# Attention with routed experts: two gathers, one copy, one eviction and the lead expert's gates stand at other places

## Chip, cores and metric

One Trainium2 chip, one core. The metric is device time in microseconds (us), the median of several runs of one launch. The engines are called as in the profile: PE is TensorE's matmul, PEld its weight load, DVE is VectorE, ACT is ScalarE, POOL is GpSimd, SP is SyncE (it only issues DMAs here).

## What is computed

A sparse attention over 8 batches, 8 heads, 576 positions and head size 64, in float32, whose output rows (4608 tokens of 512 numbers) go to one of 8 experts each.

```python
x = attention(q, k, v).transpose(0, 2, 1, 3).reshape(4608, 512)   # heads 0-3 a local mask, 4-7 a strided one
logits = x @ w_gate
e_idx = argmax(logits, axis=1)
gate_w = softmax(logits)[arange(N), e_idx]
eom = sigmoid(x @ w_output_gate)
for e in range(8):
    mask = e_idx == e
    h = maximum(x[mask] @ w1[e], 0)          # 512 -> 1024
    out[mask] = gate_w[mask, None] * eom[mask, e, None] * (h @ w2[e])
```

## The kernel before

The kernel has two parts. The first is the attention, 40 steps `t` (8 batches of `NS` = 5 steps) that run as a software pipeline: in step `t` the scores of step `t` are multiplied, the probabilities of `t - 2` are transposed, the values of `t - 3` are multiplied, and the rows of `t - 4` are transposed for the routing and written to DRAM (`xd`). Within a step the code calls `pump(place)` at numbered places; there the side work (`logits`, `gating`, `pick`, `ahead`, written as generators) goes on until it yields the next place. So the order on each engine is the order in which this Python loop issues instructions, and a waiting instruction holds up all that stand behind it on its engine.

Side work of the attention that the change touches:

- `ahead` (L475): behind batch 3 an expert is picked as the lead expert; two gathers (`fetch`, an indirect DMA that POOL issues, L157) bring 256 of its rows from `xd` into `xg`; two steps before the end of the loop PE transposes them (L497) and ACT copies them to `xe` (L500).
- `lead_layer` (L505): the lead expert's first layer on these 256 rows, 32 float32 matmuls (L530; the trace counts two records for each) in four pairs of output blocks. It serves as filler: `fill(n)` issues n of the 32. The pairs use two PSUM banks in turn; a pair is emptied by ACT (relu to `hha`, L514) and DVE (the remainder to `hla`, L515), both issued by `flush`. While `hold[0]` is true a finished pair is not emptied unless its bank is needed; after the last matmul one more call of `fill` issues the emptying of the last pair.
- `even` (L228): copies the values shifted by one block to `vev`, in quarters; the strided steps of a batch multiply with it (L334).
- `gating` (L547): routing weights, slots, and the two tables `hit` (L738, L739) and `named` (L703) from which PE makes `book` (`place`, L599; `enter`, L606). For the last batch it ends the attention: `place` of the row numbers, `tokens_first` (the indices `idx0` of the first gathers of the experts), then `weights`, `parted` (the weight in three bfloat16 parts, L696 and L698), three more `named`, `place`, `enter` and `count` (L441, L442).

The second part is `experts`. It splits the lead expert's weights in a high and a low float32r part (ACT L1003, DVE L1004), runs the second layer of the lead expert's 256 rows (`by_token`, L1124, 24 matmuls for each of two blocks of 128), then eight ranks, of which each has eight groups of layer 1 (`layer1`, L1086) and a layer 2. `gates` gives the weights of all rows, `store` scales a result by its weight on ACT (L1211) and scatters it with POOL (L1212). `rank` and `by_rank` sort the experts by load and make the indices of the gathers. A group of layer 1 writes one of four PSUM tiles `hp`; the lead expert's results stand in two tiles `yp`, which are next written in rank 0's layer 2.

Of the kernel before, what the change touches and what calls it, by code (L numbers as in the profile page):

```python
# [20 lines left out]
E = 8  # L21
# [38 lines left out]
def attn_moe_kernel(  # L60
# [111 lines left out]
    def attention():  # L172
        with ExitStack() as actx:
# [304 lines left out]
            def ahead():  # L478

                def loads():  # L480
                    for c in range(4):
                        load_w(0, 1, cs=[c])
                        yield (8, 4, 3, 0)[c]

                chains.append([loads(), clock[0] + 1, None])
                for c in range(EH // 128):
                    while now[0] % NS != 1:
                        yield 0, 3
                    xgs[c] = xg_p.tile([128, DM], F32, name="xg")
                    fetch(xgs[c], xd[0:EB * S, :], tabe[:, c:c + 1], EB * S - 1)  # L490
                    yield 0, 4 if c == 0 else 3
                for c in range(EH // 128):
                    while now[0] < ns - 2 + c:
                        yield 0, 3
                    tp = ps_g.tile([128, 512], F32, name="gp")
                    for k in range(KC):
                        nc.tensor.transpose(out=tp[:, 128 * k:128 * (k + 1)], in_=xgs[c][:, 128 * k:128 * (k + 1)],  # L497
                                            identity=ident)
                    yield 0, 4
                    nc.scalar.copy(out=xe[:, :, 128 * c:128 * (c + 1)], in_=tp.rearrange("p (k t) -> p k t", k=KC))  # L500
                    if c + 1 < EH // 128:
                        yield 0, 3
                fillers.append(lead_layer())
# [40 lines left out]
            def gating(b, j0, j1, ci):  # L544
# [191 lines left out]
                else:  # L736
                    V.tensor_tensor(out=pos[:, 1, :], in0=dst, in1=lo, op=ALU.subtract)
                    V.tensor_tensor(out=low, in0=many(lows, slice(0, n)), in1=wide(lo, 128), op=ALU.is_equal)  # L738
                    V.tensor_tensor(out=high, in0=many(highs, slice(0, n)), in1=wide(pos[:, 1, :], nh), op=ALU.is_equal)  # L739
                    for v in range(2):  # L740
                        name(v)
# [91 lines left out]
            def shifted(t):  # L833
# [6 lines left out]
                last = [(c, nc.vector, 1, 1)] if c == B - 1 and k == 2 else []  # L840
                return [(c, nc.scalar, k // 2, k % 2)] + last
# [4 lines left out]
            while t < ns:  # L846
# [40 lines left out]
                at(expo, 0)  # L887
                if t in WIPES:
                    wipe(*WIPES[t])
# [91 lines left out]
    def by_rank():  # L981
        pick = sq[:, 0].unsqueeze(2).to_broadcast([128, E, HB, E])
        page = moe.tile([128, E, HB], F32, name="page")
        nc.vector.scalar_tensor_tensor(out=page, in0=book[:, 0], scalar=float(QB), in1=book[:, 1], op0=ALU.mult, op1=ALU.add)
        for v, w in enumerate((page, gate)):
            nc.vector.tensor_tensor(out=own, in0=w.rearrange("p e k -> p k e").unsqueeze(1).to_broadcast([128, E, HB, E]),
                                    in1=pick, op=ALU.mult)
            nc.vector.tensor_reduce(out=pages[:, v], in_=own, axis=AX.X, op=ALU.add)
            if v == 0:
                nc.vector.tensor_scalar(out=pages[:, 0], in0=pages[:, 0], scalar1=float(N), scalar2=None, op0=ALU.add)  # L990
                nc.vector.tensor_copy(out=idx, in_=pages[:, 0])
# [367 lines left out]
    def experts():  # L1359
# [5 lines left out]
        gates()  # L1365
# [6 lines left out]
        by_token(0, 0, 128, lead_gate[:, 0:1], tabe[:, 0:1], lag=2)()  # L1372
# [4 lines left out]
        sent = [by_token(0, 128 * c, 128, lead_gate[:, c:c + 1], tabe[:, c:c + 1], between) for c in range(1, EH // 128)]  # L1377
        hs.append(tuple(moe.tile([128, FC, WHB], F32R, name=n) for n in ("hhb", "hlb")))
        for fn in sent:
            fn()  # L1380
        for r in range(E):
            nxt = r + 1 < E
            if r == 0:
                rank()
                by_rank()
# [8 lines left out]
            for j in range(FC):  # L1394
                layer1(r, j)
                if r == 0 and j == 1:
                    count_spare()
                    send_away()
# [117 lines left out]
```

## Time and profile before

| what | us |
|---|---|
| median of 3 runs (603.65, 604.36, 608.99) | 604.36 |
| profiled execution, whole | 609.73 |
| its span, first to last instruction | 607.8 |
| PE busy in it (96%) | 583.0 |
| DVE busy (52%) | 313.8 |
| ACT busy (46%) | 281.2 |
| POOL busy (32%) | 195.4 |

The profile is of one execution, 5.4 us above the median. A row of the timeline gives the start, the duration, the engine, the line, the operation and `out<-in` with the tiles' names, then how often it is repeated and, in brackets, how long the engine stood idle before it and what ended that. The attention fills the first 178 us, the experts the rest. From 205 us on PE is busy without a gap but for small ones near 495, 535 and 564 us, so a gap of PE before that moves the end.

### The profile page before, as it was taken

Reading aid. Unit: us, or ns where it says so; the run is one execution under the profiler, and the core shown is the slowest. Engines: PE = TensorE matmul, PEld = TensorE weight load, DVE = VectorE, ACT = ScalarE, POOL = GpSimd, SP = SyncE. Lnnn points to the kernel's source line nnn. Section 1 sums busy time; section 2 is a strip of 40 time slices with the busy share of each in tenths; the row PEclk is TensorE's granted clock in tenths of the full one; section 3 lists DMA queues with packets and bytes.
Section 4 is the critical chain, followed back from the end, with each engine's and each line's share of the span. In section 5 each row is a group of like instructions: output and inputs, shape, how many; then the busy total and the mean of one; then the engine's idle time right before and its main releaser. Section 6 shows DMA issues by size and latency. Waiting matters only on the chain. (4 is left out here: it accounts for less than half of the span.)

```text
span 607.8 us, 14522 instructions
## 1 busy us (share of the span) xinstructions
PE 583.0 (96%) x5670; PEld 492.2 (81%) x5670; DVE 313.8 (52%) x706; ACT 281.2 (46%) x553; POOL 195.4 (32%) x275
## 2 busy tenths in 40 slices
PE   7898999997989999999999999999999999999996
PEld 5676777766768989988998899889978878888875
DVE  4876989899589453443243324333532452452420
ACT  3886778786335344333333334243333442452430
POOL 4325766778321325011400140125021422311011
PEclk9998999999999999999999999999999999999998
DMA  9998898888432845053314331445055355352001
GB/s 315 315 304 262 285 294 280 262 293 252 135 126 87 324 159 175 24 171 132 121 35 163 135 121 35 148 143 149 3 184 156 94 175 142 103 179 83 19 8 52
DMA packets 42488, 97.93 MB, mean 161 GB/s; under 512 B 5458, under 2 KB 16346, under 8 KB 42394
## 3 DMA queue, kind: packets, MB, share of 16 engines
q1 hardware_dynamic: 34122, 73.47, 37.3%
q0 software_dynamic: 6864, 19.74, 9.8%
q10 hardware_dynamic: 1408, 3.38, 1.5%
q8 instruction: 71, 1.16, 0.8%
q14 instruction: 23, 0.19, 0.1%
HBM read 77.74 MB, written 20.58 MB: 162 GB/s over the span
## 5 line engine op out<-in xcount | busy, mean ns | idle before, releaser
L1086 PE MATMUL hp<-xh,w1h 128*128 128x256 f32 (+8 forms) x384 | 127.0, 331 | 1.1 <-ACTq L1292 1.1
L1086 PE MATMUL hp<-xl,w1h 128*128 128x256 f32 (+8 forms) x384 | 126.9, 331 | 0.1
L1086 PE MATMUL hp<-xh,w1l 128*128 128x256 f32 (+8 forms) x384 | 126.8, 330 | 0.0
L1124 PE MATMUL yp<-w2h,hhb 128*128 128x512 f32 (+1 forms) x208 | 83.2, 400 | 0.0
L1124 PE MATMUL yp<-w2l,hhb 128*128 128x512 f32 (+1 forms) x208 | 81.2, 391 | 0.0
L1124 PE MATMUL yp<-w2h,hlb 128*128 128x512 f32 (+1 forms) x208 | 81.1, 390 | 0.0
L1086 PEld LDWEIGHTS hp<-xh,w1h 128*128 128x128 f32 x384 | 72.6, 189 | 4.8 <-ACTq L1292 1.4
L1212 POOL DMA_INDIRECT out_dram<-ys,idx x32 | 32.9, 1030 | 132.4 <-ACT ys L1211 132.4
L1086 PEld LDWEIGHTS hp<-xl,w1h 128*128 128x128 f32 x384 | 72.6, 189 | 3.3 <-DVE xl L1004 0.4
L1212 POOL DMA_INDIRECT out_dram<-ys,ri x18 | 20.5, 1139 | 170.2 <-ACT ys L1211 167.2
L1086 PEld LDWEIGHTS hp<-xh,w1l 128*128 128x128 f32 x384 | 72.6, 189 | 2.8
L1004 DVE TENSOR_TENSOR xl<-tp,xh 128x512 fp32r<-128x512 f32 (+3 forms) x40 | 25.8, 650 | 85.4 <-ACT xh L1003 85.4
L1003 ACT CAST xh<-tp 128x512 fp32r<-128x512 f32 (+3 forms) x40 | 22.0, 556 | 99.6 <-PE tp L1063 99.6
L1109 DVE SCALAR_TENSOR_TENSOR hlb<-hp,hhb 128x384 fp32r<-128x384 f32 (+3 forms) x48 | 28.3, 591 | 67.3 <-ACT hf L1108 67.3
L1106 ACT ACTIVATE hhb<-hp 128x384 fp32r<-128x384 f32 (+3 forms) x48 | 24.8, 518 | 79.4 <-PE hp L1086 75.3
L308 POOL TENSOR_TENSOR p_t<-p_t,st 128x512 f32<-128x512 f32 x40 | 42.0, 1050 | 44.7 <-DVE rs L347 18.9
L157 POOL DMA_INDIRECT xg<-xd,idx x40 | 43.6, 1090 | 23.5 <-DVE idx L455 9.4
L1124 PEld LDWEIGHTS yp<-w2l,hhb 128*128 128x128 f32 (+1 forms) x208 | 38.8, 187 | 8.6
L1211 ACT ACTIVATE ys<-yp,pages 128x512 f32<-128x512 f32 (+1 forms) x36 | 24.9, 693 | 45.0 <-issue 35.5
L1124 PEld LDWEIGHTS yp<-w2h,hhb 128*128 128x128 f32 (+1 forms) x208 | 38.9, 187 | 8.1 <-issue 0.4
L1004 DVE TENSOR_TENSOR w1l<-raw,w1h 128x1024 fp32r<-128x1024 f32 x32 | 39.1, 1225 | 11.9 <-ACT w1h L1003 11.7
L1124 PEld LDWEIGHTS yp<-w2h,hlb 128*128 128x128 f32 (+1 forms) x208 | 38.9, 187 | 7.7
(216 smaller groups left out, 1078.7 us busy)
## 6 DMA issues: line engine op xcount, KB each, us to landing
raw<-in_moe_w_dram SPq DMA_DIRECT2D x54, 512.0 KB
vst<-in_vs_dram SPq DMA_DIRECT2D x8, 780.0 KB
vlt<-in_vl_dram SPq DMA_DIRECT2D x16, 292.5 KB
q_t<-in_ql_dram SPq DMA_DIRECT2D x8, 576.0 KB
q_t<-in_qs_dram SPq DMA_DIRECT2D x7, 650.0 KB
xd<-x_t SPq DMA_DIRECT2D x80, 54.0 KB
xd<-x_t SPq DMA_DIRECT2D x16, 256.0 KB
raw<-in_moe_w_dram ACTq DMA_DIRECT2D x6, 512.0 KB
```

What stands on the lines that cost most here:

```text
L157: nc.gpsimd.indirect_dma_start(out=dst, out_offset=None, in_=src, in_offset=bass.IndirectOffsetOnAxis(ap=idx, axis=0), bounds_check=top, o ...
L308: nc.gpsimd.tensor_tensor(out=p_t, in0=p_t, in1=st, op=ALU.subtract)
L1003: nc.scalar.copy(out=hi, in_=src)
L1004: nc.vector.tensor_tensor(out=lo, in0=src, in1=f32(hi), op=ALU.subtract)
L1086: nc.tensor.matmul(out=hp[:, 0:n], lhsT=w[:, k, 128 * j:128 * (j + 1)], rhs=x[:, k, 0:n], start=first, stop=(k == KC - 1 and w is w1l))
L1106: nc.scalar.activation(out=hh[:, j, 0:s], in_=hp[:, 0:s], func=AF.Relu)
L1109: nc.vector.scalar_tensor_tensor(out=hl[:, j, 0:s], in0=hp[:, 0:s], scalar=0.0, in1=f32(hh[:, j, 0:s]), op0=ALU.max, op1=ALU.subtract)
L1124: nc.tensor.matmul(out=yp[0:m, :], lhsT=h[:, j, o:o + m], rhs=w[:, j, :], start=(n == 0), stop=(n == len(order) - 1))
L1211: nc.scalar.activation(out=ys[0:m, 0:n], in_=yp[0:m, 0:n], func=AF.Copy, scale=w[0:m, :])
L1212: i = nc.gpsimd.indirect_dma_start(out=out.rearrange("t (k d) -> (t k) d", k=k), out_offset=bass.IndirectOffsetOnAxis(ap=row, axis=0), in_ ...
```

## The change

The change has five edits. (1) The two gathers of `ahead` stand at other places of the same step, 4 and 5 for 3 and 4. (2) The last quarter of the last batch's `even`, which was an extra copy on DVE in step 39, is made by ACT, behind the exponential of that step. (3) In the last batch's `gating` a `fill(1)` with the hold lifted stands between the table `hit` and the first two `named`. (4) `gates` and the two `store` of the lead expert are issued behind rank 0's first group of layer 1. (5) `by_rank` comes in two halves: the indices ahead of rank 0's groups as before, the weights behind its second group; `count_spare` and `send_away` move from behind the second to behind the third.

```diff
@@ ahead
                     while now[0] % NS != 1:
-                        yield 0, 3
+                        yield 0, 4
                     xgs[c] = xg_p.tile([128, DM], F32, name="xg")
                     fetch(xgs[c], xd[0:EB * S, :], tabe[:, c:c + 1], EB * S - 1)
-                    yield 0, 4 if c == 0 else 3
+                    yield 0, 5 if c == 0 else 3
@@ gating
                     V.tensor_tensor(out=high, in0=many(highs, slice(0, n)), in1=wide(pos[:, 1, :], nh), op=ALU.is_equal)
+                    if last:
+                        hold[0] = False
+                        fill(1)
+                        hold[0] = True
                     for v in range(2):
                         name(v)
@@ shifted
-                last = [(c, nc.vector, 1, 1)] if c == B - 1 and k == 2 else []
-                return [(c, nc.scalar, k // 2, k % 2)] + last
+                return [(c, nc.scalar, k // 2, k % 2)]
@@ the loop over t
                 at(expo, 0)
+                if t == ns - 1:
+                    even(B - 1, nc.scalar, 1, 1)
@@ by_rank
-    def by_rank():
+    def by_rank(v):
...
-        for v, w in enumerate((page, gate)):
...
+        w = moe.tile([128, E, HB], F32, name="page") if v == 0 else gate
@@ experts
-        gates()
         first_spare()
...
-        by_token(0, 0, 128, lead_gate[:, 0:1], tabe[:, 0:1], lag=2)()
+        sent = [by_token(0, 0, 128, lead_gate[:, 0:1], tabe[:, 0:1], lag=2)]
...
-        for fn in sent:
-            fn()
...
                 rank()
-                by_rank()
+                by_rank(0)
...
                 layer1(r, j)
+                if r == 0 and j == 0:
+                    gates()
+                    for fn in sent:
+                        fn()
                 if r == 0 and j == 1:
+                    by_rank(1)
+                if r == 0 and j == 2:
                     count_spare()
                     send_away()
```

Where it moves rows, `-` is before and `+` is the changed kernel. On POOL, in step 36 of the attention (the two gathers are L157; `named` is the table of an earlier batch):

```order
 L703 TENSOR_TENSOR named<-hit,parts 96x6x48
 L308 TENSOR_TENSOR p_t<-p_t,st 128x512
-L157 DMA xg<-xd,tabe 128x512
-L703 TENSOR_TENSOR named<-hit,parts 96x6x48 x2
-L157 DMA xg<-xd,tabe 128x512
+L703 TENSOR_TENSOR named<-hit,parts 96x6x48 x2
+L157 DMA xg<-xd,tabe 128x512 x2
 L308 TENSOR_TENSOR p_t<-p_t,st 128x512
```

The two `named` stand ahead of the first gather now, not behind it.

On DVE, in the last batch's gating (the `hit` table, an emptying L515 of the lead expert's layer, `named`):

```order
 L738 TENSOR_TENSOR hit<-hcst,lo 96x6x128
 L739 TENSOR_TENSOR hit<-hcst,pos 96x6x48
+L515 SCALAR_TENSOR_TENSOR hla<-sp,hha 128x512
 L703 TENSOR_TENSOR named<-hit,hcst 96x6x48 x2
 L606 TENSOR_TENSOR book<-book,gp 128x240
```

One emptying stands ahead of the first `named`. Some 15 rows later on the same engine, between the counts (L577, L586) and `parted` (L696, L698):

```order
 L577 TENSOR_REDUCE s_3468<-oh 96x8
 L586 TENSOR_TENSOR cum<-cum,s_3468 96x8
-L515 SCALAR_TENSOR_TENSOR hla<-sp,hha 128x512
+L515 SCALAR_TENSOR_TENSOR hla<-sp,hha 128x512 x2
 L696 CAST parts<-wall 96x6
 L698 TENSOR_TENSOR rest<-wall,parts 96x6
```

Two emptyings stand ahead of `parted` where one did; the second is that of the last pair, which before was DVE's last row of the attention. The reason is the count: the loop still calls `fill(10)` there, but one matmul has been issued earlier, so nine are left and the tenth call issues the last emptying.

On ACT, in step 39, the exponential (L312), the copy of the transposed probabilities (L325) and the gating's exponential (L618):

```order
 L425 COPY lg<-gp 128x288
 L312 ACTIVATE p_t<-p_t 128x512
+L232 COPY vev<-vlt_133 64x1040
 L325 COPY pt<-tp 128x512
 L618 ACTIVATE dd<-dd 96x48
```

The last quarter of `vev` stands between two copies of ACT; on DVE the same L232 is gone.

## Rows read from the trace of the kernel before

**Rows 1.** The page, part 1: busy us, share of the span, instructions.

```profile
PE 583.0 (96%) x5670; PEld 492.2 (81%) x5670; DVE 313.8 (52%) x706; ACT 281.2 (46%) x553; POOL 195.4 (32%) x275
```

**Rows 2.** PE's waits in the whole span: us in total, times, longest us.

```profile
PE xp L334 <- issue: 2.7, 2, 2.4
PE gp L430 <- ACT p_t L312: 2.0, 1, 2.0
...
PE sp L266 <- DMA hha<-in_ks_dram: 1.5, 1, 1.5
```

**Rows 3.** Ten-us stretches: busy us of each engine, granted clock, DMA share, GB/s.

```profile
0.00:10.00 10.00, 7.28 (x60) 5.11 (x64) 3.69 (x5) 3.52 (x3) 4.29 (x10) 1.00 0.85 265
...
40.00:50.00 10.00, 7.61 (x161) 6.05 (x163) 7.53 (x25) 4.68 (x13) 2.88 (x3) 0.91 0.83 270
...
150.00:160.00 10.00, 10.00 (x142) 7.90 (x140) 7.39 (x26) 3.08 (x10) 2.58 (x6) 0.83 0.25 73
...
170.00:180.00 10.00, 7.59 (x43) 5.89 (x42) 8.68 (x30) 2.71 (x4) 4.08 (x4) 1.00 0.30 88
```

**Rows 4.** Timeline of POOL around the two gathers: start, duration, then the instruction.

```profile
135.89 1.16 POOL L157 DMA_INDIRECT xg<-xd,tabe  x1 [0.17 <-DMA xd<-x_t]
137.09 1.29 POOL L703 TENSOR_TENSOR named<-hit,parts 96x288 bf16<-96x288 bf16 x2
138.55 1.04 POOL L157 DMA_INDIRECT xg<-xd,tabe  x1 [0.17 <-DVE rs L347]
```

**Rows 5.** Timeline of PE, 138 to 150 us.

```profile
138.43 0.78 PE L599 MATMUL gp<-named,hit 96*128 96x240 bf16 x6 [1.08 <-POOL named L703]
...
142.13 0.60 PE L497 MATMUL gp<-ident,xg 128*128 128x128 f32 x4
...
149.72 0.51 PE L430 MATMUL gp<-ident,lg 128*96 128x128 f32 x3 [2.04 <-ACT p_t L312]
```

**Rows 6.** Line L157 from 130 to 150 us: issue to landing.

```profile
DMA to landing us min/median/max: 5.7/5.8/5.9
```

**Rows 7.** DMA issues: times, then median us to landing.

```profile
xg<-xd,idx POOLq DMA_INDIRECT x40, 3.7
```

**Rows 8.** Timeline of DVE, 145 to 150 us.

```profile
145.75 2.06 DVE L232 COPY vev<-vlt 64x1040 f32<-64x1040 f32 x1
```

**Rows 9.** Timeline of ACT, 142 to 149 us.

```profile
142.77 0.58 ACT L500 COPY xe<-gp 128x512 f32<-128x512 f32 x1 [0.62 <-PE gp L497]
...
146.99 1.06 ACT L232 COPY vev<-vlt 64x1040 f32<-64x1040 f32 x1
...
148.62 0.44 ACT L425 COPY lg<-gp 128x288 f32<-128x288 f32 x1
```

**Rows 10.** Timeline of PE, 171 to 180 us.

```profile
171.79 0.43 PE L599 MATMUL gp<-named,hit 96*128 96x96 bf16 x6 [0.66 <-DVE named L703]
...
174.13 3.72 PE L530 MATMUL sp<-xe,raw 128*128 128x256 f32 x16 [0.55 <-DVE hla L515]
...
179.47 0.50 PE L1124 MATMUL yp<-w2h,hha 128*128 128x512 f32 x1 [1.21 <-ACT w2h L1003]
```

**Rows 11.** Timeline of ACT, 177 to 186 us.

```profile
177.89 0.60 ACT L514 ACTIVATE hha<-sp 128x512 fp32r<-128x512 f32 x1 [3.12 <-PE sp L530]
...
185.65 0.69 ACT L1211 ACTIVATE ys<-yp,lead_gate 128x512 f32<-128x512 f32 x1 [0.77 <-DVE spare L1262]
```

**Rows 12.** Timeline of DVE, 173 to 193 us.

```profile
173.39 0.69 DVE L515 SCALAR_TENSOR_TENSOR hla<-sp,hha 128x512 fp32r<-128x512 f32 x1
...
175.41 0.16 DVE L696 CAST parts<-wall 96x6 bf16<-96x6 f32 x1
...
176.42 1.25 DVE L703 TENSOR_TENSOR named<-hit,parts 96x288 bf16<-96x288 bf16 x3
...
179.45 2.36 DVE L1004 TENSOR_TENSOR w2l<-hhb,w2h 128x1024 fp32r<-128x1024 f32 x2 [0.18 <-ACT w2h L1003]
...
191.94 1.21 DVE L1004 TENSOR_TENSOR xl<-tp,xh 128x512 fp32r<-128x512 f32 x2
```

More of the change, by code (lines that the diff above doesn't have):

```diff
@@ L979, in gates @@
         nc.vector.tensor_reduce(out=lead_gate, in_=own[:, 0, 0:n], axis=AX.X, op=ALU.add)
-    def by_rank():
+    def by_rank(v):
         pick = sq[:, 0].unsqueeze(2).to_broadcast([128, E, HB, E])
-        page = moe.tile([128, E, HB], F32, name="page")
-        nc.vector.scalar_tensor_tensor(out=page, in0=book[:, 0], scalar=float(QB), in1=book[:, 1], op0=ALU.mult, op1=ALU.add)
-        for v, w in enumerate((page, gate)):
[L986 to L991, printed above, removed]
+        w = moe.tile([128, E, HB], F32, name="page") if v == 0 else gate
+        if v == 0:
+            nc.vector.scalar_tensor_tensor(out=w, in0=book[:, 0], scalar=float(QB), in1=book[:, 1], op0=ALU.mult, op1=ALU.add)
+        nc.vector.tensor_tensor(out=own, in0=w.rearrange("p e k -> p k e").unsqueeze(1).to_broadcast([128, E, HB, E]),
+                                in1=pick, op=ALU.mult)
+        nc.vector.tensor_reduce(out=pages[:, v], in_=own, axis=AX.X, op=ALU.add)
+        if v == 0:
+            nc.vector.tensor_scalar(out=pages[:, 0], in0=pages[:, 0], scalar1=float(N), scalar2=None, op0=ALU.add)
+            nc.vector.tensor_copy(out=idx, in_=pages[:, 0])
     def copied():
@@ L1376, in experts @@
             between[TURN_AT[c - 2]].append((split_w, 0, 1, c))
-        sent = [by_token(0, 128 * c, 128, lead_gate[:, c:c + 1], tabe[:, c:c + 1], between) for c in range(1, EH // 128)]
+        sent += [by_token(0, 128 * c, 128, lead_gate[:, c:c + 1], tabe[:, c:c + 1], between) for c in range(1, EH // 128)]
         hs.append(tuple(moe.tile([128, FC, WHB], F32R, name=n) for n in ("hhb", "hlb")))
-        for fn in sent:
-            fn()
         for r in range(E):
```

## The prediction

> **What bounds the kernel.** I read the page first: PE is busy 583.0 of 607.8 us [rows 1], and the experts' part keeps it busy nearly without a gap, so only what opens or closes a gap of PE in the attention and at its end can move the time. PE's waits come next: its longest three are 2.4, 2.0 and 1.5 us [rows 2]. Last the stretches of 10 us, for the clock: after the idle 2.4 us (at 45 us) and 2.0 us (at 148 us) the mean granted clock fell to 0.91 and 0.83, while it stayed at 1.00 in the stretch with the idle 1.5 us (at 5 us) and in that from 170 us, with three shorter ones [rows 3]. A fall is to the lower of the two levels (1.2 of 2.4 GHz); 0.83 over 10 us is 1.7 us of full clock lost. So a gap of 2 us costs its length and up to 1.7 us more.
>
> The profiled execution took 609.73 us, 5.4 above the median of 604.36. The idle 2.4 us "issue" in L334 and the lower clock behind it (together about 4 us) are what I suspect of this difference, since no tile is waited for there, but the other runs have no trace. The sum below is of differences, made on the profiled execution and then put on the median.
>
> **Edit 1, the gathers.** Before, the first gather stands at 135.89 us, the two `named` behind it end at 137.09 + 1.29 = 138.38, and PE, idle for 1.08 us, starts L599 at 138.43 [rows 4, 5]. With the `named` first (from 135.72, the gather's start less its 0.17 of idle) they end at 137.0; PE was free at 138.43 - 1.08 = 137.35, so this gap is gone. The first gather starts 1.3 us later, at 137.2; the second stays at about 138.55, and POOL is free as before. But PE needs the first gather at L497, 142.13 us. Issue to landing took 5.7 to 5.9 us here [rows 6]: it landed at 141.6, with 0.5 us to spare, and will land at about 142.9. PE, 1.08 us earlier, is there at about 141.1 and waits 1.8 us. L497 so starts 0.8 us later than before, and what was won is lost again. Bounds for the landing: the 40 later gathers of the same size took 3.7 us [rows 7], with the DMA engines mostly less loaded; that would be 140.9 and on time. I take 5.7, the row of the same two transfers.
>
> The Trainium skill, "DMA: Bandwidth & Descriptors", section "Anatomy of one DMA — SWDGE (gpsimd) path", gives 2.0 us plus bytes over 436 GB/s per DMA: by that estimate 2.6 us for these 256 KB and a landing near 140, on time. The trace does not agree: 5.7 to 5.9 us.
>
> **Edit 2, the copy.** The DVE copy takes 2.06 us at 145.75 [rows 8]. Behind it on DVE stand the normalisation, one table and L432 at 149.23, and PE's second L430 (149.72, idle 2.04) waits for L432 to free its bank, and for `lg` by ACT, 148.62 + 0.44 = 149.06 [rows 5, 9]. Without the copy L432 follows its own matmuls, near 148.5. Then `lg` is last. ACT runs without a pause from L500 (142.77, released by L497) to `lg`, so it inherits the 0.8 us: `lg` at 149.86, L430 at 149.9, that is 0.2 us later than before. The gap before it shrinks from 2.04 to 1.4 us, since the first L430 also comes 0.8 later. 1.4 us is nearer to the idles behind which the clock stayed (1.21, 1.5) than to those behind which it fell (2.0, 2.4). If it stays, most of the 1.7 us come back; some of that stretch waits for DVE, so I take 1.5. On ACT the copy takes some 1.1 us (its sister there, 1.06 [rows 9]) behind the exponential, in a pause of ACT of 1.2 us; L325 behind it ends about 0.6 late, and is needed by PE 2 us later. **Edits 1 and 2 together: +0.2 - 1.5 = -1.3 us.** Bounds: if the clock falls again behind the 1.8 us ahead of L497, +0.3; if both gaps lower it, +1.9; if the gather is on time, L497 stands where DVE frees its bank, 0.9 earlier, ACT follows, and the sum is about -2.9.
>
> **Edit 3, the reading in the gating.** The emptying ahead of `named` costs DVE 0.6 us, so the L599 of 171.79 [rows 10] starts at 172.4 (of PE's longer wait one more matmul, 0.46, fills most). The wait of 0.55 us at 174.13 for that emptying is gone, and the 32 matmuls end at 177.3 instead of 177.85. That is what is won: 0.57. What it costs is the emptying of the last pair, now ahead of `parted`. It needs ACT's L514, which needs PE's last matmul: 177.3 + 0.6 (L514, [rows 11]) = 177.9. Before, `parted` ran at 175.41, and the three `named` were done at 176.42 + 1.25 = 177.67, while PE was still multiplying [rows 12]. Now from the start of the L515 to the end of `named` it is 0.69 and then 177.67 - 175.41 = 2.26, less 0.08 in which such neighbours overlap, 2.87 together: 177.95 + 2.87 = 180.8. PE's last `place`, which followed its matmuls at once at 177.72, starts at 180.86, after 3.5 us of idle. Behind it are its own matmuls (0.5 us) and `enter` and `cnt` on DVE (another 0.5), which free the bank of L1124: 181.87 instead of 179.47 [rows 10]. The first `w2l`, before at 179.45, starts on DVE at 181.75 and is there at 182.95 (half of 2.36, [rows 12]); PE's fifth matmul wants it, and stands at 182.98; before it could not start ahead of 179.45 + 1.18 = 180.63, so it is 2.3 us later. From there a `w2l` per 1.18 us feeds six matmuls of 0.23, 1.37 us, so PE sets the pace again. **+2.3 us.** And the clock: 3.5 us idle is longer than either idle behind which it fell. A fall costs up to 1.7 us; part of it will lie in the gap or in the wait for `w2l`. I take 1.2, bounds 0 and 1.7.
>
> **Edits 4 and 5, the experts.** `gates` (four small DVE operations, 0.9 us) and the two evictions of 0.69 us [rows 11] leave a stretch in which PE is busy in both kernels. The one wait at its end is short (0.3 us ahead of layer 1, for the last `xl`, 191.94 to 193.15 [rows 12]), and its last legs are PE's transposes, ACT's cast and this DVE operation, none of which moves: I take 0, with 0.3 to be won. What they move to: behind the first group ACT's next eviction of layer 1 waits for `gates`, about 2 us longer; but four `hp` tiles of 2.2 us a group cover it (the tile is wanted at 204, and free near 201). The issue of the next weights, on ACT behind that, comes some 2 us later than 199; they are first cast at 216, and the DMA engines go quiet from 210. POOL's scatters stand behind six gathers; their buffers are four and free. The `yp` tiles are not wanted before 212. If one of these covers were gone, its lateness (about 2 us) would show at most once. I take 0.
>
> **Sum:** -1.3 + 2.3 + 1.2 = +2.2 us: 611.9 for an execution like the profiled one, 604.36 + 2.2 = 606.6 for the median.
>
> **Rivals.**
> - The clock also falls behind the late gather (idle 1.8 us, between 1.5 and 2.0, the rows that bound it): +1.6, **608.2**. For it: 1.8 is nearer 2.0. Against it: the gap is open only in so far as the landing is as late as 5.7 us.
> - Not slower: the gather is on time (as with 3.7 us): -2.9 + 3.5 = +0.6, **605.0**, and not slower than before from the point where the clock behind the gating's gap costs under 0.6 us of the 1.2 (603.8 at the least). Decides: PE does not wait for `xg` at L497. Against it: [rows 6]. By the Trainium skill's formula above it would be so.
> - The clock does not fall behind the gating's gap, since `place` and the first matmuls interrupt it: -1.3 + 2.3 = +1.0, **605.4**. Decides: granted clock 1.00 from 178 to 186 us. Against it: both longer idles of this trace lowered it.
> - Slower by more than 1%: the "issue" stall of PE, 2.4 us and the clock behind it, about 4 to 5 us (as 608.99 against 603.65), comes in the median run of the changed kernel. **611**. For it: a run of three and the profiled one seem to have it. Against it: two of three do not, and the change does not touch that place.
>
> **Chances.** Forecast 0.47, clock falls twice 0.2, gather on time 0.1, no fall in the gating 0.1, issue stall in the median 0.11; 0.02 is left for something that makes it faster by over 1%, for which I see no mechanism: even all the gaps that it touches, closed, with their clock (1.08 + 2.04 + 1.7 + 0.66 + 0.55 + 1.21), are 7.2 us, and one of them grows. A measurement of this kernel can tell about 1% (6 us) from no change. Only the stall passes it, so slower 0.11 and faster 0.02. The range reaches from 603.4, the case of the gather on time with no loss of clock (603.8) and the 0.3 of edit 4, to 610.0, the double fall with its bounds (1.9 + 2.3 + 1.7 = 5.9 at the most), and leaves out the stall and the odd rest.
>
> **What would show it.** POOL: `named` x2 ending near 137.0, then gathers at 137.2 and 138.5. PE: no wait at L599 near 138; a wait at L497 for `xg` (1.8 us; none would mean that the gather lands sooner); L430 waiting 1.4 us for ACT's `lg`, with granted clock 1.00 from 150 to 154. DVE: L515 twice in a row near 175 and 178, then `parted`. PE: no wait at L530, 3.5 us ahead of the last L599, and a lower clock behind it. If that wait is short, the main term is wrong. If ACT's L1106 or PE's layer 1 of rank 0 waits longer than now, the cover of edits 4 and 5 was gone.

## The result and the profile after

The changed kernel took 611.99 us (median of 4 runs, 610.09 to 614.95) beside 604.72 for the kernel before on the same chip: ratio 1.0116, 95% interval 1.0079 to 1.0152. It is slower by just over 1%, and 611.99 lies above the range of the prediction (603.4 to 610.0). The kernel before has a median near 605.3 over the many more runs of the experiments, 0.9 above the 604.36 on which the sum was put.

The page's first part, to be read beside [rows 1]:

```profile
PE 584.1 (96%) x5670; PEld 492.8 (81%) x5670; DVE 310.9 (51%) x705; ACT 281.3 (46%) x554; POOL 194.8 (32%) x275
```

PE does the same work. The span, 611.1 us, is 3.3 longer than before's 607.8, although before's profiled execution holds an "issue" stall of 2.4 us with a low clock behind it [rows 2, 3] and this one does not. PE's waits from 130 to 180 us (us in total, times, longest):

```profile
PE gp L599 <- DVE named L703: 4.1, 2, 3.4
PE gp L497 <- DMA xg<-xd,tabe: 1.9, 1, 1.9
PE gp L430 <- ACT lg L425: 1.4, 1, 1.4
...
```

Two of them are new, the gather (1.9) and the last `place` (3.4); the one at L430 is shorter than before (2.0). PE's timeline at these places answers [rows 5, 10] (lines behind L740 have moved by 4 or 5: L1129 is before's L1124, L1091 is L1086, L1141 is L1136, L1111 is L1106, L1216 is L1211):

```profile
137.11 0.66 PE L383 MATMUL xtp<-ident,x_t 128*128 128x128 f32 x4
139.64 0.63 PE L497 MATMUL gp<-ident,xg 128*128 128x128 f32 x4 [1.87 <-DMA xg<-xd,tabe]
...
148.27 0.53 PE L430 MATMUL gp<-ident,lg 128*96 128x128 f32 x3 [1.44 <-ACT lg L425]
...
169.31 0.43 PE L599 MATMUL gp<-named,hit 96*128 96x96 bf16 x6 [0.70 <-DVE named L703]
169.58 4.55 PE L530 MATMUL sp<-xe,raw 128*128 128x256 f32 x20
177.51 0.57 PE L599 MATMUL gp<-named,hit 96*128 96x144 bf16 x6 [3.38 <-DVE named L703]
...
178.64 0.76 PE L1129 MATMUL yp<-w2h,hha 128*128 128x512 f32 x1 [0.56 <-ACT w2h L1008]
```

The wait at L530 (0.55 us) is gone. DVE, against [rows 12], shows why the 3.38 us stand in its stead:

```profile
171.72 0.68 DVE L515 SCALAR_TENSOR_TENSOR hla<-sp,hha 128x512 fp32r<-128x512 f32 x1
174.79 0.69 DVE L515 SCALAR_TENSOR_TENSOR hla<-sp,hha 128x512 fp32r<-128x512 f32 x1 [2.40 <-ACT hha L514]
175.40 0.16 DVE L696 CAST parts<-wall 96x6 bf16<-96x6 f32 x1
...
176.27 1.18 DVE L703 TENSOR_TENSOR named<-hit,parts 96x288 bf16<-96x288 bf16 x3
```

DVE stands idle for 2.40 us in front of the last emptying, which needs PE's last matmul by way of ACT, and `parted` and the three `named` queue behind it. The stretches of 10 us (as [rows 3]: the figure right behind the five engines' busy times and counts is the granted clock, 1.00 being 2.4 GHz):

```profile
140.00:150.00 10.00, 8.50 (x109) 5.85 (x107) 4.22 (x10) 8.05 (x14) 7.04 (x14) 0.83 0.61 196
150.00:160.00 10.00, 9.76 (x151) 7.25 (x150) 7.11 (x28) 4.49 (x13) 2.80 (x9) 1.00 0.24 72
170.00:180.00 10.00, 6.07 (x30) 4.95 (x29) 6.56 (x24) 6.37 (x11) 4.05 (x4) 0.89 0.34 98
180.00:190.00 10.00, 10.00 (x38) 7.99 (x37) 6.18 (x10) 2.24 (x4) 0.00 (x0) 0.76 0.00 0
```

The clock fell to its lower level, 1.2 GHz, behind the wait for the gather (0.17 x 10 = 1.7 us of full clock lost) and behind the last `place` (1.1 + 2.4 = 3.5 us lost); it stayed behind the 1.44 us at L430.

One more thing is new, in the experts. PE's waits between 200 and 218 us, where before had none:

```profile
PE hp L1004 <- issue: 0.6, 1, 0.6
PE hp L1091 <- DVE copies L1005: 0.5, 1, 0.5
PE hp L1141 <- issue: 0.2, 1, 0.2
```

### The profile page after: what moved, and what is told of

Read it like the earlier page. It is cut to its first block, busy times and chain, and to the rows that moved or that the text cites. A ratio compares the mean times of both kernels' runs of the same rounds, so it can differ in the third digit from the quotient of the medians.

```text
span 611.1 us, 14524 instructions
## 1 busy us (share of the span) xinstructions
PE 584.1 (96%) x5670; PEld 492.8 (81%) x5670; DVE 310.9 (51%) x705; ACT 281.3 (46%) x554; POOL 194.8 (32%) x275
## 3 DMA queue, kind: packets, MB, share of 16 engines
q10 hardware_dynamic: 1408, 3.38, 1.6%
q8 instruction: 71, 1.16, 0.8%
## 5 line engine op out<-in xcount | busy, mean ns | idle before, releaser
L1091 PE MATMUL hp<-xh,w1h 128*128 128x256 f32 (+8 forms) x384 | 127.1, 331 | 1.5 <-ACTq L1297 1.1
L1091 PE MATMUL hp<-xl,w1h 128*128 128x256 f32 (+8 forms) x384 | 126.9, 331 | 0.1
L1091 PE MATMUL hp<-xh,w1l 128*128 128x256 f32 (+8 forms) x384 | 126.8, 330 | 0.0
L1129 PE MATMUL yp<-w2h,hhb 128*128 128x512 f32 (+1 forms) x208 | 83.2, 400 | 0.0
L1129 PE MATMUL yp<-w2l,hhb 128*128 128x512 f32 (+1 forms) x208 | 81.2, 391 | 0.0
L1129 PE MATMUL yp<-w2h,hlb 128*128 128x512 f32 (+1 forms) x208 | 81.1, 390 | 0.0
L1091 PEld LDWEIGHTS hp<-xh,w1h 128*128 128x128 f32 x384 | 72.6, 189 | 5.6 <-ACTq L1297 1.4
L1091 PEld LDWEIGHTS hp<-xl,w1h 128*128 128x128 f32 x384 | 72.6, 189 | 3.4 <-DVE xl L1009 0.4
L1091 PEld LDWEIGHTS hp<-xh,w1l 128*128 128x128 f32 x384 | 72.6, 189 | 2.8
L1111 ACT ACTIVATE hhb<-hp 128x384 fp32r<-128x384 f32 (+3 forms) x48 | 24.9, 518 | 80.3 <-PE hp L1091 73.4
L157 POOL DMA_INDIRECT xg<-xd,idx x40 | 43.6, 1090 | 44.1 <-DVE idx L996 22.6
L1129 PEld LDWEIGHTS yp<-w2l,hhb 128*128 128x128 f32 (+1 forms) x208 | 38.8, 187 | 8.6
L1216 ACT ACTIVATE ys<-yp,pages 128x512 f32<-128x512 f32 (+1 forms) x36 | 24.9, 693 | 45.0 <-issue 35.5
L1129 PEld LDWEIGHTS yp<-w2h,hhb 128*128 128x128 f32 (+1 forms) x208 | 38.9, 187 | 8.1 <-issue 0.4
L1129 PEld LDWEIGHTS yp<-w2h,hlb 128*128 128x128 f32 (+1 forms) x208 | 38.9, 187 | 7.7
```

The lines of the kernel that those rows point to most:

```text
L157: nc.gpsimd.indirect_dma_start(out=dst, out_offset=None, in_=src, in_offset=bass.IndirectOffsetOnAxis(ap=idx, axis=0), bounds_check=top, o ...
L1091: nc.tensor.matmul(out=hp[:, 0:n], lhsT=w[:, k, 128 * j:128 * (j + 1)], rhs=x[:, k, 0:n], start=first, stop=(k == KC - 1 and w is w1l))
L1111: nc.scalar.activation(out=hh[:, j, 0:s], in_=hp[:, 0:s], func=AF.Relu)
L1129: nc.tensor.matmul(out=yp[0:m, :], lhsT=h[:, j, o:o + m], rhs=w[:, j, :], start=(n == 0), stop=(n == len(order) - 1))
L1216: nc.scalar.activation(out=ys[0:m, 0:n], in_=yp[0:m, 0:n], func=AF.Copy, scale=w[0:m, :])
```

## The experiments

Time and ratio stand beside runs of the kernel before on the same chip (its medians there: 605.12, 605.31, 605.28 and 606.05). Executions of one kernel spread by some 2 us about their mean, so 12 runs against 23 to 35 tell about 0.25 to 0.35% (1.5 to 2 us) apart.

### The changed kernel again

No edit.

> The changed kernel once more, with more runs than the first time, beside the kernels that undo its parts. Theory A (a steady loss of about 7 us against before: 1.6 us at the late gather and 1.7 us of clock behind it, 1.7 us of stall in the gating and 3.4 us of clock, 0.7 us in the experts, less what the copy gives): about 611 us, at a ratio of 1.010 to 1.013. Theory B (the first four runs stood high by chance, since the stall, the gather's landing and the fall of the clock differ between executions): about 609 us, a ratio near 1.006, and the gather's wait at L497 missing in the profiled execution.

Measured: 611.84 us (6 runs), ratio 1.0102, interval 1.0051 to 1.0153. The loss is steady, theory A; but the profiled execution has no wait at L497, as theory B expected of it, so the late gather is no steady part of the loss. The clock behind the last `place` lost half of what it had lost in the first profile:

```profile
170.00:180.00 10.00, 6.07 (x36) 4.89 (x33) 6.50 (x26) 5.96 (x11) 4.06 (x4) 1.00 0.34 98
180.00:190.00 10.00, 10.00 (x42) 8.09 (x42) 7.08 (x12) 3.25 (x4) 0.00 (x0) 0.83 0.00 0
```

### Edit 3: undone, alone, and with nine steps of filler

Undone:

```diff
-                    if last:
-                        hold[0] = False
-                        fill(1)
-                        hold[0] = True
```

> The changed kernel without edit 3 (no reading of a pair ahead of the first named tables of the last gating); the other edits stay. Theory A (the gating's stall and the clock behind it are the main loss): the last place follows PE's matmuls at once, PE's idle 3.38 us shrinks to about 0.6, no half clock behind 178 us; 1.7 us of stall and 3.4 us of clock come back, about 606.9 us, 5 us less than the changed kernel's 612.0. Theory B (the half clock at 178 to 185 us comes from elsewhere, the late gather or the experts' moved work): the stall goes but the low clock stays, about 610 us.

Measured: 607.15 us, ratio 1.0022 (0.9988 to 1.0056); theory A to 0.3 us. PE's last `place` (L599) follows its matmuls at once again, and the granted clock is 1.00 from 170 to 190 us:

```profile
174.40 3.72 PE L530 MATMUL sp<-xe,raw 128*128 128x256 f32 x16 [0.54 <-DVE hla L515]
177.98 0.54 PE L599 MATMUL gp<-named,hit 96*128 96x144 bf16 x6
```

Alone on the kernel before (the same four lines added):

> The kernel before with edit 3 alone (the reading ahead of named, the last pair's emptying so ahead of parted). Theory A (stall of about 1.7 to 2.3 us and a fall of the clock behind it of 1.7 to 3.4 us, as in the traces of the changed kernel): 3.5 to 5.5 us more than before, about 609.5. Theory B (the clock's part is small when the other edits are gone): 2 us more, about 607.3.

Measured: 610.97 us, ratio 1.0085 (1.0056 to 1.0114), 5.1 to 5.7 us more; theory A. The wait of 3.38 us and a fall of the clock stand in its trace too.

Nine steps:

```diff
-LF = (4, 10, 4, 3)
+LF = (4, 9, 4, 3)
```

> The changed kernel with nine instead of ten steps of filler behind the counts, so that the reading ahead of named stays but the last pair's emptying stands behind the gating again, not ahead of parted. Theory A (it is the last emptying ahead of parted that costs, not the reading itself): parted follows the third emptying near 172.5 us, the named are done near 174.6, PE waits about 0.6 us at the last place, the clock stays; about 606 us, 6 us less than the changed kernel. Theory B (the reading itself costs, by its emptying ahead of the first two named): PE's waits of 0.7 and 3.4 us stay in their sum and the time stays within 1 us of 612.

Measured: 606.33 us, ratio 1.0021 (0.9991 to 1.0051); theory A. DVE and PE of this kernel:

```profile
172.24 0.68 DVE L515 SCALAR_TENSOR_TENSOR hla<-sp,hha 128x512 fp32r<-128x512 f32 x1
172.84 0.16 DVE L696 CAST parts<-wall 96x6 bf16<-96x6 f32 x1
...
175.81 0.68 DVE L515 SCALAR_TENSOR_TENSOR hla<-sp,hha 128x512 fp32r<-128x512 f32 x1
```

```profile
170.10 4.55 PE L530 MATMUL sp<-xe,raw 128*128 128x256 f32 x20
174.94 0.54 PE L599 MATMUL gp<-named,hit 96*128 96x144 bf16 x6 [0.30 <-DVE named L703]
```

The reading is still there, but the last emptying stands behind the gating, and PE waits 0.30 us instead of 3.38. So the reading costs nothing but one matmul's shift; the place of the last emptying is the loss.

### Edit 3: only its clock

Seven matmuls of zeros fill PE's idle time ahead of the last `place`; nothing reads them, and nothing else is moved.

```diff
+                        warm_up = ps_g.tile([128, 512], F32, name="gp")
+                        for _ in range(7):
+                            nc.tensor.matmul(out=warm_up[:, 0:256], lhsT=zeros[:, 0:128], rhs=zeros, start=True, stop=True)
                         enter(place(2, 2 + WP), 2, 2 + WP)
```

> The changed kernel with seven more matmuls of zeros by zeros (128x256, float32, into a bank of their own, nothing reads them) on PE ahead of the last place of the gating, about 3 us of work inside the idle 3.38 us. Theory A (PE's idle time lowers the clock): the stall of the last place stays as long, but the clock stays at 1.00 behind it; 3.4 us come back, about 608.6 us. Theory B (the low clock there has another cause than PE's idle time): no change, 612 us, or more if the added matmuls delay the place.

Measured: 607.74 us, ratio 1.0029 (1.0004 to 1.0055); 4.1 us less than the changed kernel, nearest to theory A. The zeros (L773) end 0.36 us before the `place`, which starts as late behind its matmuls as before, and the clock stays:

```profile
175.30 3.19 PE L773 MATMUL gp<-xe 128*128 128x256 f32 x14
178.84 0.54 PE L599 MATMUL gp<-named,hit 96*128 96x144 bf16 x6 [0.36 <-DVE named L703]
```

```profile
170.00:180.00 10.00, 8.44 (x48) 7.21 (x48) 6.50 (x27) 5.07 (x7) 4.05 (x4) 1.00 0.32 98
180.00:190.00 10.00, 10.00 (x48) 8.04 (x49) 8.59 (x12) 4.67 (x10) 0.00 (x0) 1.00 0.00 0
```

Work of no use ahead of a wait that was left as it is made the kernel faster: the clock falls by PE's idle time. By the traces that clock is worth 1.2 to 2.7 us (below); the 4.1 us between the medians are more, but the interval of the changed kernel's six runs is wide enough for both.

### Edit 1: undone, and alone

```diff
-                        yield 0, 4
+                        yield 0, 3
...
-                    yield 0, 5 if c == 0 else 3
+                    yield 0, 4 if c == 0 else 3
```

> The changed kernel with the two gathers of the lead expert's rows back at their places (edit 1 undone). Theory A (the late gather costs PE its wait at L497 and a fall of the clock behind it): the wait of 1.87 us goes, L599 waits some 1.1 us for named instead, no half clock at 140 us; L497 comes 1.6 us earlier and 1.7 us of clock come back: about 608.7 us, 3.3 less than the changed kernel. Theory B (the clock falls once in that stretch in any case, behind L430's wait of 1.4 to 2 us as before): only 1.6 us come back, about 610.4.

Measured: 608.62 us, ratio 1.0065 (1.0035 to 1.0096), 3.2 less than the changed kernel, as theory A had it. Its trace shows no wait at L497, 1.09 us ahead of L599 instead, and 1.00 of the clock from 140 to 160 us.

Alone on the kernel before (the diff the other way):

> The kernel before with edit 1 alone (the gathers later). Theory A (the landing differs between executions, 3.8 to 6.8 us behind the issue in the traces so far, so that PE waits for it in some executions only): 0 to 1.5 us more than before, and no wait at L497 in the profiled execution or one of up to 2 us. Theory B (a steady cost, as the 3.2 us by which the changed kernel without edit 1 is shorter): 3 us more, about 608.3.

Measured: 606.61 us, ratio 1.0026 (0.9999 to 1.0053): 1.3 to 1.6 us more, between the theories and nearer to A. For the mechanism the landing rows tell more than the times. The two gathers of the changed kernel's first profile, which have no landing on record (the first is issued at 132.8 us and PE gets it at 139.64, 6.8 us later), and the landings of three other kernels with edit 1 (the changed one without edit 3, with nine steps, with the zeros):

```profile
L157 POOL DMA_INDIRECT xg<-xd,tabe x2: 1013/1090/1167, 132.8 to 134.3; - x2
```

```profile
DMA to landing us min/median/max: 4.2/5.2/6.3
```

```profile
DMA to landing us min/median/max: 3.8/5.6/7.4
```

```profile
DMA to landing us min/median/max: 4.1/5.7/7.3
```

Of the eight traces with edit 1 the profile names the gather as the end of a wait in two: 1.87 us (first profile) and 0.68 (edits 1 and 2, below). It ends waits in three more. With edit 1 alone the first gather lands at 139.77 us and L497 starts 0.13 us behind that, as it does behind the landing in the trace with 0.68; DVE's L589, which reads the bank that L497 writes next, had ended 0.55 us earlier, so the name in the first row is not what PE waited for. It is the same without edit 3 and with the zeros, where PE stands idle for 0.17 and 0.09 us. The second row is an idle for which the profile names no tile, about 5 us behind L497; the row below is what the DMA queue q8, called "instruction", moved between 142.5 and 142.6 us, a packet of 16 KB that lasts from 142.52 to 143.89:

```profile
139.90 0.63 PE L497 MATMUL gp<-ident,xg 128*128 128x128 f32 x4 [0.43 <-DVE book L606]
...
145.48 0.63 PE L337 MATMUL xp<-vst,pt 64*64 64x65 f32 x13 [2.38 <-issue]
```

```profile
q8 instruction: 1, 0.02, 85.8%
```

Such an "issue" idle in L337, between 144 and 146 us, stands in five of the eight traces with edit 1 (1.24, 1.32, 1.80, 2.21 and 2.38 us) and in none of the eight without it. In the five the packet ends 1.2 to 1.6 us ahead of the matmul behind the idle; in the eight without edit 1 the last packet before that same matmul ends 2.3 us or more ahead of it, and in the three with edit 1 and no idle 1.4 us or more.

### Edit 2 alone, and edits 1 and 2 together

Edit 2 on the kernel before:

> The kernel before with the last quarter of the even copy on ACT behind the last exponential (edit 2 alone). Theory A (the step of the prediction: PE's wait at the second L430 shrinks from 2.04 to about 1.4 us and the clock does not fall behind it): 1.5 to 2 us less than before, about 603.3 us. Theory B (the clock falls behind the wait all the same, or falls in few executions of before): 0 to 0.6 us less.

Measured: 603.47 us, ratio 0.9962 (0.9933 to 0.9990): faster, theory A. PE's wait at the second L430, and the clock of the two stretches around it:

```profile
145.03 0.53 PE L430 MATMUL gp<-ident,lg 128*96 128x128 f32 x3 [1.43 <-ACT lg L425]
```

```profile
140.00:150.00 10.00, 8.51 (x137) 6.43 (x133) 7.73 (x26) 8.75 (x18) 7.42 (x14) 1.00 0.51 170
150.00:160.00 10.00, 9.76 (x116) 6.87 (x109) 5.20 (x16) 3.38 (x9) 4.08 (x10) 1.00 0.53 161
```

Edits 1 and 2 on the kernel before:

> The kernel before with edits 1 and 2 together and no other. Theory A (their effects add up: 1.3 us for the gathers and -1.85 us for the copy, each alone): about 604.8 us, 0.5 less than before. Theory B (the prediction's sum of -1.3 us, the gather's delay being hidden by the copy's gain): about 604.0. Theory C (they do not add up: without the copy on DVE, PE reaches L497 earlier and waits longer for the gather, with a fall of the clock behind it in some executions, as the 3.2 us by which the changed kernel is shorter without edit 1): 606.5 or more.

Measured: 604.84 us, ratio 1.0005 (0.9980 to 1.0030) beside a median of before of 606.05. By the ratios the two alone add up to -0.12% (1.0026 and 0.9962), so this is theory A within the interval. Theory C, 1.2 us more than before (1.0020), is not borne out by the median but lies inside the interval too, and B, 1.3 us less (0.9979), lies at its edge. The 3.2 us of edit 1 within the changed kernel were not found again here.

### Edits 4 and 5

Undone in the changed kernel (the part of the diff from `by_rank` on):

> The changed kernel with the lead expert's gates and evictions and the weights half of by_rank back at their places (edits 4 and 5 undone). Theory A (they cost only PE's two new gaps of 0.57 and 0.46 us at 208 and 212 us, of which before had about 0.3): 0.7 us less than the changed kernel. Theory B (they are a main part of the loss, by ACT's longer issue of the next weights): 2 us less or more.

Measured: 608.48 us, ratio 1.0049 (1.0019 to 1.0079), 3.4 less than the changed kernel: theory B by the time. PE has no wait at all between 180 and 216 us.

Alone on the kernel before:

> The kernel before with edits 4 and 5 alone (gates, evictions and weights half behind rank 0's first groups). Theory A (the traces: PE's new waits for a free hp tile, about 1.0 us together, since ACT's evictions stand behind gates and a longer issue of the next weights): 1 us more than before, about 606.2. Theory B (the 3.4 us by which the changed kernel without them is shorter are their steady cost): 3 us more, about 608.4.

Measured: 607.25 us, ratio 1.0028 (1.0006 to 1.0050), 1.7 to 2.0 more, between the theories. PE's waits from 180 to 212 us:

```profile
PE hp L1136 <- issue: 1.4, 1, 1.4
PE hp L1086 <- issue: 0.2, 1, 0.2
```

Edit 5 alone (`by_rank` in halves, `count_spare` and `send_away` a group later):

> The kernel before with edit 5 alone (by_rank in two halves, count_spare and send_away one group later; gates and the lead expert's evictions as before). Theory A (the waits for hp come from ACT's evictions behind gates, edit 4): no change, within 0.4 us of before, and no wait of PE between 200 and 215 us. Theory B (they come from DVE's work of by_rank behind the second group): 1 us more and the same waits.

Measured: 606.48 us, ratio 1.0020 (0.9997 to 1.0043). The time is not told apart from no change nor from 1 us more, nor from edits 4 and 5 together (1.0028); the trace shows no wait of PE of 0.15 us or more between 180 and 218 us, as theory A had it.

Edits 4 and 5 with `gates` back at its old place, so that only the two evictions and the halves are moved:

```diff
         for c in range(4):
             split_w(0, 2, c)
+        gates()
         first_spare()
...
-                    gates()
                     for fn in sent:
```

> The kernel before with the lead expert's two evictions behind rank 0's first group and by_rank in halves, but gates at its old place. Theory A (ACT's evictions of layer 1 are late because the lead expert's evictions wait there for gates): the waits of PE for hp between 204 and 215 us are mostly gone, at most 0.3 us more than before by the trace, about 605.6 us. Theory B (the two evictions themselves, 1.26 us of ACT, and the later issue of the next weights are enough to use up the four hp tiles): about 1 us of waits of PE there, and about 607 us as with gates moved too.

Measured: 605.86 us, ratio 1.0008 (0.9982 to 1.0034); theory A, though the interval meets that of edits 4 and 5 with `gates` moved too (1.0006 to 1.0050). PE waits 0.2 us:

```profile
PE hp L1136 <- issue: 0.2, 1, 0.2
```

ACT shows what `gates` delays. In the kernel before, the issue of the next weights (L166) and the eviction behind it; then the same in the changed kernel, behind the lead expert's two evictions (L1216) that wait for `gates` (`own`, L982); then the two evictions with `gates` early:

```profile
199.09 1.92 ACTq L166 DMA_DIRECT2D raw<-in_moe_w_dram  x4
201.05 0.57 ACT L1106 ACTIVATE hhb<-hp 128x480 fp32r<-128x480 f32 x1 [2.56 <-DVE away L1150]
```

```profile
200.02 1.26 ACT L1216 ACTIVATE ys<-yp,lead_gate 128x512 f32<-128x512 f32 x2 [2.13 <-DVE own L982]
201.18 0.57 ACT L1111 ACTIVATE hhb<-hp 128x480 fp32r<-128x480 f32 x1
201.41 0.37 ACTq L166 DMA_DIRECT2D raw<-in_moe_w_dram  x1
...
201.95 3.10 ACTq L166 DMA_DIRECT2D raw<-in_moe_w_dram  x3
205.10 0.57 ACT L1111 ACTIVATE hhb<-hp 128x480 fp32r<-128x480 f32 x1 [3.24 <-PE hp L1091]
```

```profile
189.31 1.27 ACT L1211 ACTIVATE ys<-yp,lead_gate 128x512 f32<-128x512 f32 x2
```

### The two edits that help

Edit 2 and edit 3 with nine steps, on the kernel before:

> The kernel before with edit 2 (the copy) and the reading of edit 3, with nine instead of ten steps of filler behind the counts, so that the last pair's emptying stays behind the gating; gathers and experts as before. Theory A (edit 3 costs by the place of the last emptying alone, and brings 0.6 us with that mended, while the copy brings 1.5): about 602.5 us, faster than before by some 2.5. Theory B (the copy's clock does not come back): about 604.5.

Measured: 603.02 us, ratio 0.9963 (0.9932 to 0.9993). It is faster than the kernel before, and so than the changed one, and is not told apart from edit 2 alone (0.9962). From the last L430 to the first matmul of the lead expert's second layer its trace is 0.77 us shorter than that of edit 2 alone (12.53 against 13.30).

## Why the prediction was wrong, and where it held

The edits, each alone on the kernel before, add up by their ratios: 0.26% (edit 1), -0.38% (edit 2), 0.85% (edit 3), 0.28% (edits 4 and 5), together 1.01%, or 6.1 us; the changed kernel has 1.02 and 1.16%. Undone one at a time in the changed kernel, edits 1, 3, and 4 with 5 give back 0.37, 0.80 and 0.53% of its 1.02%; against 0.26, 0.85 and 0.28% alone, that is within the intervals. So nothing is lost by the edits' meeting that these times could show, and the sum can be gone through term by term. A table by stage says the same without the attention's own spread; each column is the time from the first matmul of one kind to that of the next, from PE's timeline (the 5.85 us from the first `tp` to layer 1, alike in all, are left out):

| us | last L430 to second L599 | to `yp` (before's L1124) | to first `tp` (L1063) | layer 1 of rank 0 to its layer 2, and on to the end |
|---|---|---|---|---|
| before | 5.62 | 7.68 | 7.29 | 19.16 + 396.00 |
| changed, first profile | 6.10 | 9.33 | 9.73 | 20.54 + 396.29 |
| changed, second | 6.10 | 9.29 | 8.57 | 20.99 + 395.56 |
| edit 3 alone | 6.10 | 9.29 | 8.31 | 19.28 + 396.18 |
| changed, with zeros | 6.10 | 9.29 | 7.06 | 19.38 + 397.31 |
| changed, nine steps | 6.10 | 6.43 | 7.49 | 19.18 + 396.61 |

**Edit 3, the stall: right.** Forecast: 0.57 us won, one matmul moved ahead, an idle of 3.5 us ahead of the last `place`, 2.3 us in all. Measured: 0.48 later at the second L599 (the moved matmul), an idle of 3.38, then 1.61 more to `yp`; with the clock kept (zeros) 0.23 of it comes back in the next column. That is 1.9 us.

**Edit 3, the clock: right in kind, its bound too low.** Forecast 1.2, at most 1.7. The third column exceeds before's 7.29 by 1.0 to 2.4 us, and by 0.23 more against the one with zeros, so 1.2 to 2.7. In all five traces with the 3.38 us the clock fell; in three it lost 1.7 us by the ten-us stretches, in two 3.4 to 3.5. The bound was read off two falls behind idles of 2.0 and 2.4 us [rows 3] and taken for a longest one; the longest in the 16 traces, behind an "issue" idle of 2.21 us in the changed kernel without edit 3, lost 5.1 us (0.68 and 0.81 in the stretches from 140 and 150 us). Stall and clock are together 3.1 to 4.6 us by the traces; the times, 0.85% alone, say 3.4 to 6.9. The forecast was 3.5: near the lower end of both.

**Edit 2: the wait right, the clock's return taken too surely.** L430 waits 1.43 us for `lg` and the clock stays behind it in all nine traces with a wait of 1.43 or 1.44 there. But what came back was read off one execution. Of the five traces in which the copy is on DVE and PE waits 1.9 to 2.1 us at L430, the clock fell in two (before, edit 3 alone) and stayed in three. So the "1.5 that come back" would have come back in two of these five executions. From the first L497 to the last L430 it is 22.5 to 22.6 us with the copy on DVE and no fall, 24.0 to 24.1 with one, and 21.9 in the four shortest traces with the copy on ACT: 0.6 us from the copy, 1.5 more where the clock would have fallen. (The other six with the copy on ACT all have edit 1 and took 22.6 to 27.8 us; see there.) The time, -0.38%, is in keeping with that.

**Edit 1: the landing is no number but a spread, and another idle came with it.** The step "I take 5.7" rested on one pair. From issue to landing the pair took between 3.8 and 7.4 us. PE waited 0.7 us or less for the first one in seven of the eight traces, so that the rival "the gather is on time" describes most executions to within that; the late gather with a fall of the clock describes the first profile, where it cost 1.87 and about 1.7 us. The Trainium skill, "DMA: Bandwidth & Descriptors", section "Anatomy of one DMA — SWDGE (gpsimd) path", by whose formula 2.6 us were estimated, would have put it in time always. No trace here shows so short a landing: the shortest of this pair is 3.8 us, that of the 40 later gathers 2.7. What edit 1 costs in the mean is 0.26%, 1.6 us, with an interval that reaches to nothing. That an in-time gather should have won (the rival's -2.9 for edits 1 and 2) was wrong: the two together came out at 1.0005. What takes that gain back, as far as the traces show, is an idle that the prediction did not have: the "issue" idle in L337, 1.2 to 2.4 us in five of the eight traces with edit 1 and in none of the eight without it, with a fall of the clock at two of the five. It is longer than the 1.08 us that are won at L599. It looks like a wait of PE for its own instructions (see the last section), whose packet comes later with edit 1; no run tests that, and why it comes later is open.

**Edits 4 and 5: wrong, the step that failed.** The text named the cover, "four `hp` tiles of 2.2 us a group cover it", and took 0. Counted from layer 1 of rank 0 to the end, the seven traces with both edits take 415.6 to 417.1 us, and the nine others, all with `gates` at its old place, 414.7 to 415.5; the means are 416.4 and 415.1, so 1.35 us, where 0 was taken and about 2 told as the price of a lost cover. With `gates` early and all else moved it is 415.24, with edit 5 alone 415.36. So the loss goes with the place of `gates`; by the times alone these kernels are not told apart.

How the loss comes about is shown for the first profile. There `gates` makes ACT 2.13 us late (L1216), as the text had it. The issue of the next weights behind it was taken to come 2 us later at its old length, but it took 3.47 us (0.37 + 3.10), where before it took 1.92. So the third eviction of layer 1, 5.46 us behind the first before, comes 7.90 behind it (205.10). DVE's share of it follows at 205.82, then `count_spare` and `send_away` (206.39 to 208.18), which edit 5 put there, and only then the emptying of the fourth group. PE's L1004 writes that group's tile; it starts 0.06 us behind the emptying's end, though the profile calls its wait "issue":

```profile
208.08 0.65 DVE L1114 SCALAR_TENSOR_TENSOR hlb<-hp,hhb 128x480 fp32r<-128x480 f32 x1
```

```profile
208.79 0.69 PE L1004 MATMUL hp<-pages,ident 128*64 128x96 f32 x12 [0.57 <-issue]
```

So ACT's delay and DVE's moved work together use up the tiles: 1.0 us with the wait for `copies` behind it. The second profile has 0.6 us of the kind and the one with the zeros 0.1. In the other four of the seven no wait of PE ends with a tile there: the cover held. With edits 4 and 5 alone the third eviction comes 6.89 us behind the first (6.63 with `gates` early), ACT is back at before's pace from the fifth on, and PE's 0.2 and 1.4 us come 6 and 11 us later as "issue", with no tile that is late. An "issue" idle among these matmuls (before's L1136), 0.1 to 1.4 us, stands in eight of the nine traces with edit 5 and in none of the seven without it, so a part of the loss may be edit 5's. It ends 1.5 to 1.6 us behind a packet of the queue q8, like the idle at L337; the packet ends 19.9 to 21.3 us behind the first matmul of layer 1 in the seven traces with `gates` moved, and 18.9 to 19.8 in the nine others. What makes it late is open.

**The sum.** Edits 1 and 2: -1.3 forecast, -0.7 from the two alone and +0.3 together, with 1.5 us of doubt. Edit 3: 3.5 forecast, 3.1 to 4.6 by the traces, 5.1 by the time. Edits 4 and 5: 0 forecast, 1.35 by the traces, 1.7 by the time. All three went the same way. The base was 0.9 us low as well (604.36 of three runs, 605.3 of many). The upper end of the range was added up 0.3 us short (604.36 + 5.9 is 610.3, not 610.0), which does not change that the time lies above it. The rival that ended above 1%, an "issue" stall in the median run, is not what happened: the changed kernel's first profile has no such stall, and it is slower all the same. But idles of that kind came at other places, with edits 1 and 5, where the text had looked for none.

## To carry to other kernels

An instruction that is moved ahead of others by a count (`fill(1)` there, ten steps here) also moves the end of its sequence: look what the last call of the count now stands in front of; here one step less (nine for ten) gave back as much as leaving the edit out (1.0021 and 1.0022). A price of the clock or of a DMA read off one execution is one draw; take it times its share of executions where the idle is short, and no bound of it for an idle that is longer than those seen. Where an engine's evictions are made to wait, add every DMA issue that the engine has queued behind them, at more than its old length, and the work of the other engine that empties the same buffers, before calling them a cover. And look through several executions for idles for which no tile is late: a change of order can bring them at places that it does not touch.

## What the runs showed of the hardware

How often the clock falls goes with how long PE stood idle, but not strictly. In 16 traces, of PE's idles of 1.0 to 1.6 us (86) none was followed by a fall, of those of 1.6 to 1.9 us (9) two, of those of 1.9 to 2.4 us (13) eight, and of those of 3.38 us (5) all (the idle at the start of the span is left out). Two idles of the same length and place, 2.04 us ahead of L430, show it: in the kernel before the granted clock behind it (150 to 160 us) was 0.83 [rows 3], in the one with edits 4 and 5 alone, where it ends at 144.69 us, the clock stayed at 1.00:

```profile
140.00:150.00 10.00, 7.90 (x130) 6.01 (x125) 8.84 (x24) 6.82 (x15) 6.77 (x13) 1.00 0.45 148
```

Seven matmuls that nobody reads, in an idle of 3.4 us, kept the clock at 2.4 GHz and brought more than they cost. And the same four DMA issues on ACT took 1.92 us at one place and 3.47 at another.

PE's "issue" idles have a sign in the traces. All 31 of them of 0.6 us or more, in the 16 traces, end 1.25 to 1.62 us behind the end of a 16 KB packet of the DMA queue that the profile calls "instruction" (71 or 72 such packets in some 605 us). So PE seems to stand there without instructions; no run tests it. A shorter one can hide a tile: PE's 0.57 us at L1004 ended 0.06 us behind DVE's emptying.
